# Another order of the same items in a fused gated-delta-rule and softplus kernel on one core

## The chip, the core and the metric

The kernel runs on one core of a Trainium2 chip. The metric is device time in microseconds: the median of several executions. Five instruction streams matter: PE (TensorE), DVE (VectorE), ACT (ScalarE), POOL (GpSimd) and SP (the queue that issues most loads). Each runs its own list strictly in the written order and waits where an operand is not ready or a buffer not free.

## The reference

Two layers follow each other. The first is a linear attention with a delta rule, for 4 batches x 8 heads, 768 time steps, head size 48; the second a feed-forward layer on 3072 tokens of 384 features with 2048 hidden units.

```python
k_n = k / (norm(k) + 1e-6)
for t in range(768):
    y[t] = g[t] * einsum('bhd,bhde->bhe', q[t], state)
    v_old = einsum('bhde,bhd->bhe', state, k_n[t])
    state = state + beta[t] * einsum('bhd,bhe->bhde', k_n[t], v[t] - v_old)
x = y as (3072, 384)
h = x @ w_in
out = (maximum(h, 0) + log1p(exp(-abs(h)))) @ w_out
```

## The kernel before

**Chunks.** Time is cut into 12 chunks of 64 steps. All 32 (batch, head) pairs of a chunk are worked on together. Within a chunk the recurrence is solved by a triangular inverse; between chunks only the state goes on. Chunks are paired into six groups (0 and 1, 2 and 3, and so on), and one inverse serves a pair.

**Items.** The kernel first records a list of 1286 items. An item is a small piece of work on one engine with its dependences and buffers: a load, a group of matmuls, a copy. A word in the table `_ORDER` then names an engine letter (P PE, D DVE, A ACT, G POOL, S SP) and the item's number, and `emit` issues the items exactly in that order. Buffers come from rings and are given out in the order of first use, so the order also sets which buffer an item waits for. Nothing else decides the order: there is no scheduler behind it. The names of items used below, with c for the chunk:

- `load` (lines 302 and 305): k, q, v or g of a chunk in two halves of 192 KB each, all issued by SP. The twelve buffers of one ring take them. `bload` (264) are small loads of beta, `wload` (330) the four parts each of w_in and w_out, issued by POOL and cast on the way.
- `cast` (copies at 209 to 213) makes f16 of q and of the first chunks' k; `ksq` and `red` (351 to 362) square k and sum it; `sqrt` or `pow` (368 to 374) and `eps` (381, 383) finish the norms; `kmul` (406) scales k by them.
- `trsk`, `trsq` (422, 454) transpose k and q on PE; `kev`, `qev` copy the result out (tile kqt). `gram` (516) and, for chunks 0 and 1, `gramd` (540), `gramk` and `gramq` form the products k k' and q k'; `kkc` copies and `mask` (498, DVE) take them out into tiles kk and mt.
- The inverse of a pair: `ln` and `pick` (604, 627; 597 for the first pair), `prep` (644), 15 `step`s (656 to 671) on DVE or POOL one behind the other, `ca` and `cb` (686, 688), three transposes `st.a`, `st.b`, `st.c` (714, tiles dn, td, tb), `tx`. Then per chunk `xmm` (744), `xs` (753), `tmm` (768), `td2`, `zmm` (789), `z`.
- The chain over chunks: `ks`, `qs` (826: old state times k and q), `w` (866: v minus that), `umm` (880), `u1`, `zu` (893), `u2`, `smm` (910) with `s` (924: the new state), `ymm` (936) with `y` (950: times g), `ytr` (963: transposes) and `xt` (copy of the result to the dense layer's input).
- The dense layer: `g1` (989) is a group of products of x with w_in, `soft` (1001) the softplus on ACT, `g2` (1016) four products with w_out, `o` the copy of an output tile, `store` (1035) its two stores.
- `fill` (1046): a group of four 128x512 products of the identity whose result nobody reads. The prediction calls it a warming group. 40 are recorded and 13 are in the table.

**Small and dense.** Most products of the chunks are small (48 to 64 rows and columns), the dense ones use the whole array. There are 96 `g1` and 96 `g2` groups, which the table puts between the small ones. PSUM has five buffers for the chunks' products, two for `g1` and a single one for `g2`, so a next output tile can start only when `o` has copied the last one out.

**Which engine.** Many items may go to one of several engines, and the letter in the table says which. So the table sets not only when a copy or a step runs but also where.

Of the kernel before, what the change touches and what calls it, by code (L numbers as in the profile page):

```python
# [1066 lines left out]
S26 S25 P138 P161 S33 S34 P151 A12 G4 S44 A173 S43 G2 A169 D176 P177 P174 D0 G227 A178 P188 D170 A15  # L1067
A3 S29 G1 D175 P182 A189 A171 D204 S30 S49 A190 A197 D183 P205 D206 S36 G201 A11 P158 S35 S28 D184
G9 D198 P202 G280 D203 D172 P281 A199 D200 D225 P216 G714 P210 A211 A212 G715 D226 P141 A282 P185
A187 A7 S27 S60 S59 S52 D5 P213 A217 A10 A207 S51 S50 A218 A179 P180 A214 A181 A186 G228 D229 D230  # L1070
S22 P208 A209 D231 D232 G233 D234 D235 D236 P133 S32 S24 A215 S41 D237 D238 D239 D240 D241 D242 D243
D244 D245 D248 D246 A293 D250 S23 S42 G273 A368 P369 S57 A370 S66 P145 P194 P136 P255 A247 A249 S31
S58 S17 D196 P264 D251 D195 S18 D257 A254 D256 G253 P258 A300 G8 D252 G121 D265 A260 P301 P135 G123
D294 S20 D266 S19 D274 G6 A259 P261 P716 A13 A295 A262 A263 A717 A718 P191 D192 A275 S21 P719 A720
S38 S37 D193 D302 D721 P147 A713 G122 D16 P219 S65 G315 G14 G361 G126 P725 D221 G125 D220 P722 D727
D726 G316 P728 D296 P137 D276 D297 D277 A724 A723 A729 P934 P928 A935 A929 D362 G363 P298 D299 P926
A927 S40 P278 D279 P303 A304 P308 A310 A309 P930 D306 D305 P283 A284 A285 P936 D307 D312 D364 P288
A931 D311 G365 D287 D292 P731 P932 A289 A290 A937 S39 D291 D286 D313 G124 P366 P267 A268 A269 G730
P150 P270 S67 S45 A933 D314 G317 G318 D733 A381 G319 G320 A367 D732 S46 D382 P735 A737 A736 D272
D271 P949 P950 D321 D322 G127 G323 P222 D224 P734 S68 D223 D324 D325 S73 P738 P938 A739 A740 P744  # L1080
A939 D326 D745 P940 G327 P371 P741 D746 D328 P747 G128 P164 S81 D742 A748 G329 A372 S99 D743 A941
G330 P951 D374 P970 A373 D331 P376 A388 P956 A971 G332 D379 D380 P749 D375 S74 G333 A378 D334 P958
A377 A957 D751 G383 A959 D336 P964 D338 A337 P389 S82 A335 P962 A390 D339 G342 P952 A965 S48 P343
D384 P352 S76 A341 D345 D344 G385 A953 D750 D340 P960 P346 A449 A348 S84 P942 A961 S47 A963 D347
D354 P753 A754 P349 A469 S75 P966 D450 D351 G451 A350 D755 D353 P968 S83 A967 P386 D470 S100 S98
D387 P752 P756 D758 P943 D757 G471 S53 D452 P391 A393 S54 P944 D392 A954 D395 P762 D394 D764 P396
A397 A955 P759 D760 A398 P945 D761 A946 D401 S97 P355 P972 G403 G453 A356 A969 P454 G476 S55 A357
P973 D763 A455 S56 P765 D402 G404 G405 D400 P974 A766 D399 G406 P767 A456 P358 D769 P975 G407 A360
D768 G408 P457 D359 A976 A978 S977 P770 G409 D458 G410 P771 A772 P979 S105 D773 A557 P477 D411 P774
G412 D775 A776 S62 P980 A564 D472 P780 S61 G413 A478 P777 D781 P981 D782 G414 A947 D473 P783 A784  # L1090
P459 P982 D460 D461 P992 A983 D462 D778 P474 S64 A993 P1008 D558 S92 A475 P1000 D779 A1009 P464 S89
D463 P479 A1001 P986 D468 A481 S113 D482 A466 D483 P990 D480 G415 G491 G416 G417 G418 G419 A987 D465
G420 P785 A991 D467 P988 D786 D787 P1012 G421 A989 S71 P484 G559 D424 A423 P998 S114 D422 A1013 D488
S90 D426 P1025 A485 A425 P996 P440 A486 D427 A999 P431 A997 S70 P994 G579 P1002 G645 S91 D489 A995
G430 P1004 A1003 S80 D433 A429 P1026 D432 G492 A1005 D490 G493 G494 P434 S106 A985 D428 S63 P1006
A436 A435 P1014 G495 D441 A1007 D442 P437 A1015 P789 S948 G496 G497 D438 P1010 A537 D790 D487 P1016
A439 D791 A1011 P1027 G498 D538 S69 A1017 P788 D560 P1028 G539 D499 P792 A1029 D500 P565 A793 D794
P1018 A566 D501 P795 D797 A1031 P798 P1019 G502 A1030 D800 D799 A625 P443 G561 P1020 D796 A444 D540
A445 G503 P801 P1021 D646 G504 P446 A1022 P803 D448 P1032 A802 S1024 G505 G506 D447 S72 D804 P562
S94 D805 P1033 A563 D626 P807 A809 D808 A544 P806 S79 P1034 G507 P810 P1035 A811 S115 D508 D509 D512  # L1100
A812 D511 P545 A1036 P816 A546 D510 P813 S78 D817 P1039 S107 G541 A513 D818 P572 A573 D815 P819 D576
S77 P1040 G647 A820 D575 D514 P542 A574 P1048 A543 P1060 D814 D580 A1049 D515 P547 P567 A1061 P1066
D551 A568 D550 G517 A569 D570 P1068 A1067 G518 S1037 D549 P552 G627 P1062 A1069 A548 S116 P1058 D556
D571 D554 D553 S85 A1063 D577 D578 P821 A1038 P519 P1052 A1059 P1072 S108 A1053 S86 S112 S96 P1041
A1073 P1056 A1057 D581 P1064 S87 G582 D521 G583 G584 P1042 D823 D822 A1065 P1050 D520 G585 D516
P1046 G586 A1051 P522 P528 D555 P1054 A523 D529 A524 A1047 D587 D628 P525 P825 A1043 S1045 D530 S95
# [56 lines left out]
```

## Time and profile before

| what | value |
|---|---|
| median of 3 runs | 243.78 us (242.98 to 243.94) |
| span of the profiled execution | 241.5 us |
| PE busy | 219.4 us (91%), 5020 matmuls |
| DVE busy | 161.7 us (67%) |
| ACT busy | 152.8 us (63%) |
| POOL busy | 113.7 us (47%) |
| moved by DMA | 27.57 MB, mean 114 GB/s |

The profile shows one execution. The span reaches from its first to its last instruction; the times of the runs are longer by what lies around it, and for the profiled execution itself only the span is listed. In rows of groups and of the timeline, L12 is line 12 of the kernel, "x32" a count, and what stands in square brackets is the idle time of the engine ahead of the row with what ended it. The line of a copy is that of a helper (209 for ACT, 211 and 213 for DVE and POOL), so copies are told apart by their tiles.

### The profile page before, as it was taken

How to read it: one execution, taken by the hardware profiler on the slowest of the kernel's cores; microseconds unless marked ns; L12 is line 12 of the kernel's file. 1: busy time of each engine (PE TensorE's matmuls, PEld its weight loads, DVE VectorE, ACT ScalarE, POOL GpSimd, SP SyncE). 2: the span in 40 equal slices, each digit the busy share in tenths (PEclk: the TensorE clock that was granted, in tenths of full speed). 3: DMA queues.
4: the chain of work that ended last, by engine and by line, in shares of the span. 5: the costliest groups of instructions: out<-in, count | busy, mean ns of one | idle time of the engine just before them, and what ended most of it. 6: DMA issues, size and time to landing. Idle time of an engine off the chain costs nothing.

```text
span 241.5 us, 11396 instructions
## 1 busy us (share of the span) xinstructions
PE 219.4 (91%) x5020; PEld 135.6 (56%) x5020; DVE 161.7 (67%) x368; ACT 152.8 (63%) x292; POOL 113.7 (47%) x197
## 2 busy tenths in 40 slices
PE   7645877879988999999999999999999999999983
PEld 2423455646764664556655566655565555677751
DVE  2768699888897889987899757896496310623000
ACT  5767576764982778876895767757363674143540
POOL 8740393875779778989597482016620000000000
PEclk9985599999999999999999999999999999999999
DMA  6999989999999399961889514962302311303112
GB/s 102 182 245 137 167 135 190 176 173 180 180 217 167 57 177 164 162 113 35 150 153 184 97 30 94 160 122 52 69 21 52 68 34 25 64 19 81 35 33 65
DMA packets 86833, 27.57 MB, mean 114 GB/s; under 512 B 77048, under 2 KB 86776, under 8 KB 86784
## 3 DMA queue, kind: packets, MB, share of 16 engines
q1 hardware_dynamic: 80624, 20.83, 52.6%
q0 software_dynamic: 3840, 3.17, 8.5%
q10 hardware_dynamic: 2320, 2.85, 5.2%
q8 instruction: 39, 0.64, 1.2%
q14 instruction: 10, 0.08, 0.1%
HBM read 25.26 MB, written 4.72 MB: 124 GB/s over the span
## 4 chain that ended last, share of the span: by engine, by line
PE 75%; DMA 7%; DVE 6%; SPq 4%; issue 3%; ACT 2%; POOL 1%; DVEq 0%; ACTq 0%; POOLq 0%
PE o L1016 27%; PE h L989 26%; DMA w_in<-in_moe_w_in_dram 4%; PE d L826 3%; SPq L305 3%; PE d L936 3%; PE d L516 2%; DMA f<-in_q_dram 2%; PE d L422 2%; PE d L963 2%; PE d L454 2%; PE d L880 2%; PE d L910 2%; PE d L893 2%; PE d L768 1%
## 5 line engine op out<-in xcount | busy, mean ns | idle before, releaser
L1016 PE MATMUL o<-w_out,ga 128*128 128x384 f16 x384 | 77.7, 327 | 0.7 <-ACT osb L209 0.6
L1001 ACT ACTIVATE ga<-h 128x512 f16<-128x512 f32 x96 | 56.5, 599 | 29.8 <-PE h L989 25.9
L989 PE MATMUL h<-xt,w_in 128*128 128x512 f16 (+1 forms) x384 | 74.0, 327 | 0.5 <-DMA w_in<-in_moe_w_in_dram 0.3
L989 PEld LDWEIGHTS <-w_in 128*128 128x128 f16 x384 | 34.5, 98 | 21.2 <-DMA w_in<-in_moe_w_in_dram 0.8
L1016 PEld LDWEIGHTS <-ga 128*128 128x128 f16 x384 | 33.7, 98 | 21.8 <-issue 0.8
L664 POOL TENSOR_TENSOR tmp<-nn,tt 128x78 f32<-128x78 f32 (+7 forms) x53 | 19.2, 362 | 16.1 <-DVE tt L671 13.0
L373 POOL TENSOR_TENSOR nv<-nv,half_c 128x16 f32<-128x16 f32 x8 | 23.5, 2940 | 6.6 <-DVE nv L362 6.5
L671 POOL TENSOR_TENSOR tt<-tt,tmp 128x78 f32<-128x78 f32 (+7 forms) x53 | 20.4, 385 | 4.2
L498 DVE TENSOR_TENSOR mt<-d,mask 128x256 f16<-128x256 f32 x48 | 18.2, 413 | 4.5 <-PE d L516 3.5
L209 ACT ACTIVATE kqt<-d 128x1024 f16<-128x1024 f16 (+1 forms) x18 | 18.0, 1000 | 4.8 <-PE d L454 3.6
L211 DVE CAST u<-d 128x384 f16<-128x384 f32 x20 | 10.9, 554 | 14.3 <-PE d L880 7.9
L209 ACT ACTIVATE u<-d 128x384 f16<-128x384 f32 x28 | 13.0, 490 | 11.8 <-PE d L880 5.4
L1046 PE MATMUL h<-ident 128*128 128x512 f16 x52 | 18.1, 493 | 1.7 <-DVE ident L197 1.7
L209 ACT ACTIVATE kk<-d 128x256 f16<-128x256 f32 x37 | 13.4, 386 | 6.3 <-PE d L516 5.4
L209 ACT ACTIVATE osb<-o 128x384 f32<-128x384 f32 x19 | 9.3, 492 | 9.4 <-PE o L1016 9.3
L454 PE MATMUL d<-ident,qn 128*128 128x128 f16 x96 | 8.5, 243 | 6.7 <-ACT qn L209 5.9
L950 DVE TENSOR_TENSOR yg<-d,f 128x384 f16<-128x384 f32 x24 | 12.3, 551 | 2.9 <-PE d L936 2.8
L924 DVE TENSOR_TENSOR s<-s,d 128x384 f16<-128x384 f16 x20 | 10.4, 542 | 5.7 <-PE d L910 4.3
L644 POOL TENSOR_TENSOR nn<-ln,beta_l 128x256 f32<-128x256 f16 x8 | 6.1, 780 | 14.2 <-DVE ln L627 14.2
L209 ACT ACTIVATE xt<-d 128x768 f16<-128x768 f16 x10 | 8.1, 813 | 7.0 <-PE d L963 7.0
L866 DVE TENSOR_TENSOR w<-f,d 128x384 f16<-128x384 f32 x22 | 11.3, 545 | 1.4 <-ACT xt L209 0.7
L362 DVE TENSOR_REDUCE nv<-f 128x16 f32<-128x768 f32 x12 | 11.3, 942 | 1.0 <-ACT f L351 1.0
(117 smaller groups left out, 346.7 us busy)
## 6 DMA issues: line engine op xcount, KB each, us to landing
f<-in_k_dram SPq DMA_DIRECT2D x24, 192.0 KB, 5.7
f<-in_q_dram SPq DMA_DIRECT2D x24, 192.0 KB, 5.6
f<-in_v_dram SPq DMA_DIRECT2D x24, 192.0 KB, 5.3
f<-in_g_dram SPq DMA_DIRECT2D x24, 192.0 KB, 5.3
out_dram<-osb ACTq DMA_DIRECT2D x29, 96.0 KB, 2.7
out_dram<-osb SPq DMA_DIRECT2D x19, 96.0 KB, 2.8
w_in<-in_moe_w_in_dram POOLq DMA_DIRECT2D x4, 384.0 KB, 7.9
w_out<-in_moe_w_out_dram POOLq DMA_DIRECT2D x4, 384.0 KB, 8.4
```

The costliest lines, as they stand in the source:

```text
L209: nc.scalar.activation(o, x, AF.Copy, scale=float(sign))
L362: lambda en: nc.vector.tensor_reduce(nvs().rearrange("p (a h) -> p a h", a=2), ksq.ap, mybir.AxisListType.X, ALU.add),
L373: nc.gpsimd.tensor_tensor(nvs(), nvs(), half_c[:, :NU], ALU.pow)
L454: nc.tensor.transpose(o[:, j], qn.ap[:, j].rearrange("p m d -> p (m d)"), ident)
L498: nc.vector.tensor_tensor(mt[c][m].ap[:, NP * p : NP * p + NP], gb[m].ap.rearrange("p (i b) -> p i b", i=NP)[:, :, n : n + C], mask[:, Non ...
L664: ENG[en].tensor_tensor(t, nn.ap[:, :, j : j + 1, j + 1 :].broadcast_to([P, 2, w, n]), tt.ap[:, :, :w, j : j + 1].broadcast_to([P, 2, w, n ...
L671: ENG[en].tensor_tensor(rows, rows, t, ALU.add)
L950: lambda en, m=m: nc.vector.tensor_tensor(heads(yg.ap, m), hd(yp[m].ap), heads(gf.ap, m), ALU.mult),
L989: nc.tensor.matmul(hp.ap[:, n * b : n * b + n], w_in[:, j, f * P : (f + 1) * P], xt.ap[:, j, t0 : t0 + n], start=(j == 0), stop=(j == 2),)
L1001: lambda en, hp=hp, o=gb: nc.scalar.activation(o.ap, hp.ap, AF.Softplus),
L1016: nc.tensor.matmul(op.ap[:, :DM], b.ap[:, col + c0 : col + c0 + 128], w_out[:, f, :], start=(f == 0), stop=(f == NF - 1),)
L1046: nc.tensor.matmul(hp.ap, ident, ident[:, None, :].broadcast_to([P, 4, P]))
```

## The change

Only the table is replaced. Both tables name the same 1259 items, each once (27 warming groups are left out), 13 warming groups among them. Rows of the old and of the new table around the start, around the first dense groups and at the end:

```diff
-S26 S25 P138 P161 S33 S34 P151 A12 G4 S44 A173 S43 G2 A169 D176 P177 P174 D0 G227 A178 P188 D170 A15
-A3 S29 G1 D175 P182 A189 A171 D204 S30 S49 A190 A197 D183 P205 D206 S36 G201 A11 P158 S35 S28 D184
+P147 G13 D11 D2 P138 A1 S25 D0 P161 G10 G227 G16 S26 G9 A173 D176 P174 P150 P177 S44 A169 A3 A175
+A14 A4 A12 D170 D178 S34 S33 P182 D201 P202 D204 A197 D198 A171 A203 P205 P145 A206 P210 A199 A184
...
-P150 P270 S67 S45 A933 D314 G317 G318 D733 A381 G319 G320 A367 D732 S46 D382 P735 A737 A736 D272
+A272 G365 G126 D292 G317 G318 G319 P222 D223 D224 P932 P731 D733 D732 S45 P734 P735 A381 A929 A736
...
-P1260 A1261 S1210 P1242 A1255 P1256 A1254 P1243 A1257 P1264 P1244 A1265 P1266 P1245 A1267 P1262
-A1246 A1247 P1272 A1263 P1270 A1248 P1273 A1271 P1268 A1269 P1274 P1275 A1276 A1277 A1278 P1279
-P1280 P1281 P1282 A1283 S1285 A1284
+P1256 A1261 A1257 P1243 P1264 S1204 S1254 P1244 P1266 A1265 A1255 P1245 P1262 A1267 A1246 A1248
+A1263 P1272 P1270 P1273 P1268 P1274 A1271 A1269 P1275 A1165 A1164 A1276 A1277 S1278 S1247 P1279
+P1280 P1281 P1282 A1283 A1284 S1285
```

What it comes to, read from the two tables:

- **Loads on SP.** Before: k0, k1, q2, v0, half of k3, q1, q0, q4, q3, and so on. After: k0, half of q2, k1, q0, v0, a beta load, halves of q4, g0, q2, k5, k2, q4, k3, q1, k4, then the second half of q1 (the 20th load), k3, q3, k2, g0, q3, k4.
- **Warming groups.** Before: nine ahead of `zu` of chunk 0, one (number 18 of the 40) right behind it, one behind `ytr` of chunk 0, and two among the dense groups (behind `tmm` and `ytr` of chunk 1). After: twelve ahead of `zu` of chunk 0, and one behind `ymm` of chunk 0.
- **Around the first dense group.** Before, `trsk` and `gram` of chunks 3 and 2 stand between the first `g1` groups. After, both `trsk` and `gram` of chunk 3 stand ahead of the first `g1` group; the copy `xt` of chunk 0 goes from ACT to DVE.
- **Engines.** DVE has 42 of the 90 steps instead of 32, POOL 48 instead of 58; DVE has 17 `kkc` copies instead of 11, 7 `xt` instead of 2, 5 `z` instead of 10; ACT has 20 stores instead of 29, SP 28 instead of 19.
- **Later on** the sequence on PE is nearly the same, with neighbours exchanged.

More of the change, by code (lines that the diff above doesn't have):

```diff
@@ L1072 @@
[L1072 to L1076, printed above, removed]
@@ new lines @@
+P1066 D548 A513 D516 D570 D571 P1068 A1067 A549 A1069 P821 P1052 P1058 A1053 P552 A1059 D823 P519
+D553 D515 P1062 P1050 A1063 P1042 P1046 D521 D520 D518 D822 A1051 A554 A652 D555 D556 D577 A1047
+P1056 A1043 A1057 G517 P528 P522 P1072 A1073 A524 P1064 S93 D529 D523 D530 S101 S1038 S80 S79 P1085
+A1065 P525 P825 A527 S87 S85 S104 S119 D578 P1054 S1037 S103 A526 D826 D579 P531 P824 A1055 P1076
+S977 A827 A1077 G647 G627 D532 D628 P1070 P828 A830 G580 D581 D582 G583 G584 G585 D667 A632 G586
+P1086 P1074 D533 D829 P831 D832 P834 D836 D648 D833 D835 A1075 A1071 A1045 P1087 D668 P633 P1088
```

109 lines of the change are left out of this document (54 added, 55 removed).

## Prediction

> **What bounds the kernel now.** I read the page first (its slices of the span), then the busy time by stretches, and then the timeline of the stretches that are not full. The first fence is from the page: clock granted to PE and DMA share, in tenths, 40 slices of 6 us.
>
> ```profile
> span 241.5 us, 11396 instructions
> ...
> PEclk9985599999999999999999999999999999999999
> DMA  6999989999999399961889514962302311303112
> ```
>
> ```profile
> 12.00:24.00 12.00, 6.41 (x141) 3.82 (x138) 9.20 (x33) 8.62 (x16) 2.47 (x5) 0.70 1.05 192
> 24.00:36.00 12.00, 9.88 (x255) 5.63 (x256) 9.47 (x19) 7.94 (x17) 7.76 (x10) 0.73 0.98 149
> 48.00:60.00 12.00, 10.19 (x306) 6.99 (x305) 10.49 (x26) 6.14 (x13) 8.14 (x16) 1.00 1.12 174
> 60.00:80.00 20.00, 17.99 (x502) 12.80 (x500) 17.51 (x35) 14.26 (x30) 16.23 (x18) 1.00 1.14 187
> 80.00:100.00 20.00, 19.91 (x482) 11.81 (x481) 17.87 (x38) 15.90 (x28) 16.17 (x34) 1.00 0.79 129
> 120.00:140.00 20.00, 19.98 (x445) 10.68 (x446) 16.84 (x39) 15.22 (x31) 14.73 (x22) 1.00 0.87 142
> ```
>
> The second is the busy time by stretches. Columns: stretch, length, busy time of PE, weight loads, DVE, ACT, POOL, clock, DMA share, GB/s. There are two regimes. From 80 us PE is busy 19.9 to 20.0 of every 20 us: PE itself is the bound, and an order with the same products can gain nothing there, only lose by a new wait. Before 80 us PE is not full, and the first dense group starts only at 40.5 us (its row stands below); there loads (DMA share about 1.0 from the start) and the chain of the first two chunks through ACT and DVE set the pace. So the change has to be priced at the start, and watched afterwards.
>
> **The change, part by part.** Every item appears once in both tables, with the same 13 warming groups, so the work removed and added is nothing; the tail (last four output groups, two last stores) stands in the same order. The profiled execution has a span of 241.5 us; the median of the runs is 243.78, so about 2.3 us lie around the span, in both kernels.
>
> *Loads.* Almost all loads stand at other places. What they cost is seen where the casts wait:
>
> ```profile
> 6.09 0.52 ACT L209 ACTIVATE kn<-f 128x384 f16<-128x384 f32 x1 [2.24 <-DMA f<-in_k_dram]
> 18.36 0.84 ACT L209 ACTIVATE qn<-f 128x768 f16<-128x768 f32 x1 [0.21 <-DMA f<-in_q_dram]
> 19.26 1.89 PE L454 MATMUL d<-ident,qn 128*128 128x128 f16 x16 [3.86 <-ACT qn L209]
> 26.88 1.32 ACT L686 ACTIVATE tw<-tt,mx 128x512 f16<-128x512 f32 x2
> 27.91 1.89 PE L1046 MATMUL h<-ident 128*128 128x512 f16 x4
> 28.45 1.06 DVE L714 STREAM_TRANSPOSE tb<-tw 128x512 uint32<-128x512 uint32 x1
> 29.73 0.96 PE L744 MATMUL d<-dn,kk 64*64 64x32 f16 x64
> ```
>
> The first two loads land at 6.1, the 13th (q of chunk 0) at 18.4: (18.36 - 6.09) / 11 = 1.11 us a load. In the new order q of chunk 1 is complete only with the 20th load, at about 18.4 + 7 x 1.11 = 26.1, and ACT now has its cast (0.84) directly ahead of the two copies that let the first inverse out (1.32). So these end at 26.1 + 0.84 + 1.32 = 28.3, where they end at 28.2 now, although the 15 steps of that inverse are all on DVE in the new order. The transpose st0.c starts at 28.4 as before. On PE, trsq1 (eight of the 16 products that take 1.89) runs from 27.0 to 28.0 and a warming group stands between it and xmm0; in the slow clock that group takes 1.89 us, so xmm0 starts at 29.9 (now 29.73). No gain up to here.
>
> *From xmm0 to the first dense group.* More stands in the queues of this chain:
>
> ```profile
> L209 ACT ACTIVATE kqt<-d 128x1024 f16<-128x1024 f16 (+1 forms) x18 | 18.0, 1000 | 4.8 <-PE d L454 3.6
> ...
> w_in<-in_moe_w_in_dram POOLq DMA_DIRECT2D x4, 384.0 KB, 7.9
> ```
>
> ```profile
> 26.91 1.47 POOL L353 TENSOR_TENSOR f<-f 128x768 f32<-128x768 f32 x1 [9.52 <-DMA f<-in_k_dram]
> 37.72 1.02 DVE L950 TENSOR_TENSOR yg<-d,f 128x384 f16<-128x384 f32 x2
> 39.34 1.76 DVE L406 TENSOR_TENSOR kn<-f,nv 128x768 f16<-128x768 f32 x2
> 39.34 0.81 ACT L209 ACTIVATE xt<-d 128x768 f16<-128x768 f16 x1 [0.46 <-PE d L963]
> 40.51 1.49 PE L989 MATMUL h<-xt,w_in 128*128 128x256 f16 x12 [0.34 <-DMA w_in<-in_moe_w_in_dram]
> 41.01 0.95 DVE L362 TENSOR_REDUCE nv<-f 128x16 f32<-128x768 f32 x1
> 43.58 0.69 DVE L211 COPY kqt<-d 128x1024 f16<-128x1024 f16 x1 [0.41 <-PE d L422]
> ```
>
> ACT has the copy qevq1 (1.0) ahead of td20, and DVE a transpose and a cast ahead of xs1: I put umm0 1.0 us later. The products of y0 end now at 37.72 + 1.02 = 38.7; with that 1.0 and a mask that stands between them (0.4) at 40.1. Copy xt0 goes from ACT to DVE, behind kmul2.0 (half of 1.76), red4 (0.95) and kevk2.0 (0.69): 40.1 + 0.9 + 0.95 + 0.7 + about 0.5 for itself gives 43.1, where it ends at 40.15 now. On PE the transposes of chunk 2 stand ahead of ytr0 and wait for the same kmul2.0. The first dense group starts at about 43.2, 2.7 later. Its weights come just ahead: on POOL the second w_in load stands behind the square of k4 (26th load, 18.4 + 13 x 1.11 = 32.8, and 1.47), is issued near 34.3 and takes 7.9: 42.2.
>
> *From there to umm1.* The late part is mostly work brought forward (trsk3, trsk2 and gram3 already stand before the first dense group), so I compare at umm1, which both need for chunk 1.
>
> ```profile
> 47.48 1.93 DVE L604 STREAM_TRANSPOSE ln<-kk 128x1024 uint32<-128x1024 uint32 x1
> 47.72 0.83 PE L989 MATMUL h<-xt,w_in 128*128 128x256 f16 x6
> 48.38 0.61 PE L422 MATMUL d<-ident,kn 128*128 128x128 f16 x8
> 49.29 1.04 PE L1046 MATMUL h<-ident 128*128 128x512 f16 x4
> 50.09 1.01 DVE L866 TENSOR_TENSOR w<-f,d 128x384 f16<-128x384 f32 x2
> 52.24 0.43 PE L880 MATMUL d<-w,td 64*64 64x48 f16 x31 [0.92 <-ACT kqt L209]
> 54.01 0.32 PE L516 MATMUL d<-kqt 48*64 48x64 f16 x16
> 54.16 0.42 PE L826 MATMUL d<-s,kqt 48*64 48x48 f16 x32
> ...
> 58.68 1.03 PE L1046 MATMUL h<-ident 128*128 128x512 f16 x4
> ```
>
> ```profile
> L498 DVE TENSOR_TENSOR mt<-d,mask 128x256 f16<-128x256 f32 x48 | 18.2, 413 | 4.5 <-PE d L516 3.5
> L213 DVE TENSOR_SCALAR kk<-d 128x256 f16<-128x256 f32 x11 | 4.3, 415 | 0.4 <-PE d L516 0.4
> ```
>
> DVE has from xt0 to w1.0: ten masks (10 x 0.413), three kk copies (3 x 0.415), ln2 (1.93), pick2 and eps4 (about 0.9), w1 (1.01), together about 9.2; w1.0 ends at 43.1 + 9.2 = 52.3 and umm1 at about 52.9, now 52.24 + 0.43 = 52.7. That is +0.2 to +0.3. By then PE has done one dense group (0.83) and one transpose group (0.61) less, but gramq1.1 and qs1 (0.32 + 0.42) more: +0.7. The two warming groups at 49.29 and 58.68 are gone from here (2.1 us), but the first stood in a wait: its time becomes waiting. Sum at umm1: +1.0.
>
> *53 to 80 us.* Here PE now waits 20.00 - 17.99 = 2.0 us between 60 and 80, and spends 1.03 in the second warming group. This cover can absorb the 1.0; against it stands an inverse of chunks 2 and 3 that comes out about as late as now (its ln2 starts near 47.5 in both). I take -0.5, between -1.0 and 0.
>
> *After 80 us.* SP gets nine more stores and ACT nine fewer, and SP's loads stand behind those stores, which wait for their output copies. The tightest pair I find is v of chunk 10, behind the stores of chunk 7's first output; its use by w10 stands a full chunk of dense groups later. I count 0, and nothing for the issue time that ACT saves, since PE does not wait for ACT there. DVE is the tight one: it gets 42 of the 90 steps instead of 32.
>
> ```profile
> 121.54 1.08 DVE L714 STREAM_TRANSPOSE dn<-ta 128x512 uint32<-128x512 uint32 x1
> 127.44 1.92 DVE L604 STREAM_TRANSPOSE ln<-kk 128x1024 uint32<-128x1024 uint32 x1
> ...
> 163.06 0.42 DVE L753 TENSOR_TENSOR xs<-d,mk 128x256 f16<-128x256 f32 x1
> ```
>
> ```profile
> 164.02 0.18 PE L768 MATMUL d<-tb,xs 64*64 64x32 f16 x2
> ```
>
> ln8 now starts 5.9 us after st6.a. In the new order 16 items stand between them (two transposes, six masks, three kk copies, two w, two xs, a tx): with the means above 9 us, so ln8 starts near 132 instead of 127.4. Followed down the DVE and POOL columns, the last xs8 then ends near 164.0, where it ends at 163.5 now and PE uses it at 164.02. The half microsecond of slack is gone: I take +0.3, from 0 to +4, because several such places follow one another.
>
> *The spreading.* From chunk 1's first dense group on, the places where a dense group follows a small product or a transpose number 83 in the old order and 82 in the new. I count nothing for it.
>
> Sum: +1.0 - 0.5 + 0.3 = +0.8, so 243.78 + 0.8 = **244.6 us**, practically no change.
>
> **The rivals.** *Faster, 242.2.* The clock column shows 0.70 and 0.73 between 12 and 36 us, after a wait of PE of 3.86 us (row of 19.26 above). In the new order twelve of the 13 warming groups stand before zu0 (now nine) and the longest wait of PE there is, by my column sums, 2.4 us (trsq2 waits for q2). If the clock then stays full, the group ahead of xmm0 takes 1.04 instead of 1.89 and the start loses 0.45 less; if the waits between 60 and 80 and the group at 58.68 go as well (2.0 + 1.0, of which I count 0.5 already), the sum is +0.8 - 0.45 - 2.0 = -1.6. [...] Against it: PE would still be mostly idle between 22 and 27 us in the new order, and between 24 and 36 us the mean clock was only 0.73 although PE was busy for 9.88 of 12 us, so a wait much shorter than 3.86 does not make it safe.
>
> *Slower, 247.* The DVE column after 120 us. Point from which it decides: xs8 later than 164.0, or o5.1, which is now on DVE behind the last step of inverse 8, later than 154. Each microsecond beyond goes into PE; at +3 the time is 247.
>
> *Slower, 246.* The loads: 1.11 us a load is one estimate, and q of chunk 1 is the 20th. At 1.25 it lands 1.0 us later, and the whole first chain with it; with waits for k4 and for the weights behind it +2.
>
> *The change doesn't do what it says:* the dense part is nearly the same sequence, so this is the forecast itself.
>
> **How the numbers follow.** Forecast 0.42 (own range 243.4 to 245.8), faster rival 0.22, DVE 0.24, loads 0.12. I take 0.5% (1.2 us) as what a measurement can tell. Below 242.6: 0.22. Within: 0.30 of the forecast's 0.42. Above 245.0: 0.12 + 0.24 + 0.12 = 0.48. The range, 241.5 to 248.5, reaches to the faster rival less 0.7 and the DVE rival plus 1.5.
>
> **What would show it.** First dense group at 43.2 (right: 42 to 44); umm1's end at 52 to 53.5; PE busy about 10 us of the 12 from 48 to 60, with no warming group among them; DVE's ln8 near 132; PE at 20.0 of 20 in each stretch from 80 to 220 (waits ahead of L768 or L880 there are the DVE rival). A granted clock of 1.00 between 12 and 36 is the faster rival. Wrong altogether: a first dense group before 40 or after 46.

## The result, and the profile after

The changed kernel takes **251.18 us** (250.35 to 251.40, four runs) against 243.86 us of the old one on the same chip (242.98 to 244.07): a ratio of 1.032 (95% interval 1.027 to 1.037). The forecast was 244.6 with a range that ended at 248.5. The profiled execution took 250.99 us with a span of 249.2 us. In some kernels below the runs of one order lie up to 7 us apart, the longer ones mostly at a lower granted clock (a3: 247.18 us at 0.979, 253.03 to 254.05 at 0.939 to 0.952), so every range is given and the ratios rest on the shorter runs alone.

The first lines are from the profile's page of the changed kernel: the granted clock and the DMA share in 40 slices, and one row of the DMA queues (packets, MB, share) that the prediction never looked at.

```profile
span 249.2 us, 11387 instructions
...
PEclk9989558979999999999999999999999999999999
DMA  6999999999991399980599984920101600021123
...
q8 instruction: 39, 0.64, 1.3%
```

The busy time by stretches, columns as in the prediction (stretch, length, busy time of PE, weight loads, DVE, ACT, POOL, clock, DMA share, GB/s):

```profile
24.00:36.00 12.00, 8.31 (x168) 4.87 (x167) 10.31 (x17) 6.28 (x14) 8.78 (x10) 0.54 1.18 150
48.00:60.00 12.00, 8.87 (x251) 6.21 (x250) 9.16 (x24) 6.44 (x16) 9.14 (x10) 0.86 1.34 192
60.00:80.00 20.00, 17.40 (x481) 12.98 (x481) 16.47 (x40) 13.95 (x26) 9.97 (x15) 1.00 0.91 148
80.00:100.00 20.00, 18.60 (x498) 11.88 (x492) 17.27 (x40) 14.57 (x29) 15.12 (x28) 1.00 0.70 123
140.00:160.00 20.00, 18.46 (x555) 11.70 (x544) 14.25 (x36) 9.16 (x18) 14.11 (x30) 1.00 0.79 143
```

PE is less busy than before from 24 to 36 us (8.31 against 9.88) and from 48 to 60 us (8.87 against 10.19), and, against the forecast, it is not full between 80 and 100 and between 140 and 160 us either. What ends PE's waits is in its timeline (start, length, operation, count; in brackets the wait ahead of the row and what ended it):

```profile
35.12 1.03 PE L454 MATMUL d<-ident,qn 128*128 128x128 f16 x8 [1.31 <-DVE qn L211]
...
43.81 0.24 PE L910 MATMUL d<-u,kn 64*64 64x48 f16 x5 [0.78 <-issue]
...
46.21 0.82 PE L989 MATMUL h<-xt,w_in 128*128 128x256 f16 x6
...
50.83 0.72 PE L989 MATMUL h<-xt,w_in 128*128 128x256 f16 x5 [1.38 <-issue]
...
57.30 0.21 PE L826 MATMUL d<-s,kqt 48*64 48x48 f16 x1 [1.64 <-issue]
...
63.49 0.40 PE L910 MATMUL d<-u,kn 64*64 64x48 f16 x25 [2.07 <-issue]
...
92.16 0.46 PE L936 MATMUL d<-u,mt 64*64 64x48 f16 x18 [1.10 <-issue]
...
145.32 0.59 PE L989 MATMUL h<-xt,w_in 128*128 128x512 f16 x2 [0.80 <-issue]
...
149.88 0.30 PE L789 MATMUL d<-td,kk 64*64 64x32 f16 x15 [0.74 <-issue]
```

Two things stand here. The first dense group starts at 46.2 instead of 40.5 (forecast 43.2). And from 43 us on each of PE's long waits ends with "issue": no operand was late that the profile shows. They lie in the middle of a group, ahead of its last product even (row of 57.30). The reader can find out what they have in common by counting. A window that reaches from the end of one such wait to the end of the next gives PE's products and its own weight loads (its LDWEIGHTS records):

```profile
43.81:50.83 7.02, 5.02 (x128) 3.60 (x129) 7.02 (x16) 4.11 (x11) 5.71 (x5) 1.00 1.16 193
50.83:57.30 6.47, 4.83 (x129) 3.27 (x129) 3.94 (x9) 2.36 (x5) 3.90 (x6) 0.74 1.33 198
57.30:63.49 6.19, 4.12 (x128) 3.18 (x128) 4.08 (x15) 4.13 (x8) 5.51 (x8) 1.00 1.37 177
92.16:149.88 57.72, 55.88 (x1409) 32.71 (x1409) 49.55 (x108) 42.01 (x81) 39.60 (x65) 1.00 0.82 142
```

128 + 128 = 256 each time (one or two more where an edge counts twice), and 2818 = 11 x 256 + 2 over the long stretch. Queue q8 moves 0.64 MB in 39 packets, 16.4 KB each; PE's 5020 products and 5020 weight loads are 39 times 256 and a rest, so there is about one packet for 256 of them. I call such a block of 256 of PE's instructions a **page** and the place between two of them a page edge; that a packet of q8 is the fetch of the next page is my reading of these counts and of the times below. In the list of all of PE's records, counted from 0 and with the two to four records of its sequencer that stand ahead, the first product behind each wait has number 1218, 1474, 1730, 1986, 3522, 6081 and 6337 (another run can have the same edge one record earlier or later). Over 0.4 us there are no other waits of PE between 36 us and the last output group; together these seven are 8.5 us of a span of 249.2. The old kernel has two such waits at the same spacing (0.58 and 0.76 us, at 1473 and 2753):

```profile
47.53 0.25 PE L826 MATMUL d<-s,kqt 48*64 48x48 f16 x9 [0.58 <-issue]
...
73.02 0.35 PE L893 MATMUL d<-u,z 64*64 64x48 f16 x21 [0.76 <-issue]
```

When a page comes late is seen in the packets of q8. In the view of the DMA queues (packets, MB, share of the 16 engines in the window) the page needed at 49.4 us has not begun until 48.2 us, although the page before it began at 43.81; loads fill the engines:

```profile
q0 software_dynamic: 542, 0.50, 69.6%
q1 hardware_dynamic: 1055, 0.33, 40.0%
```

```profile
q0 software_dynamic: 197, 0.15, 80.8%
q1 hardware_dynamic: 186, 0.09, 38.7%
q8 instruction: 1, 0.02, 5.5%
```

(The first fence is 43.81 to 48.2 us, the second 48.2 to 49.4; q0 carries the loads of w_in and w_out that POOL issues, below "loads of the weights", q1 the loads that SP issues.) Taken for several pages from the same packets and from PE's records:

| kernel, page at number | page before began | fetch began (later by) | PE ran on | PE's wait |
|---|---|---|---|---|
| before, 1473 | 41.06 | 45.08 (4.02) | 47.53 | 0.58 |
| before, 1729 | 47.53 | 48.58 (1.05) | 53.43 | 0 |
| before, 1985 | 53.43 | 53.89 (0.46) | 57.74 | 0 |
| after, 1474 | 43.81 | 48.28 (4.47) | 50.83 | 1.38 |
| after, 1730 | 50.83 | 54.41 (3.58) | 57.30 | 1.64 |
| after, 1986 | 57.30 | 60.77 (3.47) | 63.49 | 2.07 |

In these rows a fetch starts only after the page before has begun, and where PE waits it runs on 2.4 to 2.9 us after the start of the fetch. In the last three rows PE had used up the page before 5.64, 4.83 and 4.12 us after it began, sooner than the delay and this time together (7.02, 6.47 and 6.19).

**The sum.** Products of `ymm0` end 3.1 us later (40.8, before 37.7). Behind that, page waits grow by 8.51 - 1.34 = 7.2, PE's other waits over 0.4 us fall from 3.15 to 0, and two warming groups fewer stand there (2.1). 52.3 to 55.7 us run at half clock with PE busy (rows below), about 1.7 by my estimate, half of that stretch. 3.1 + 7.2 - 3.15 - 2.1 + 1.7 = 6.8 of the 7.7 us of the spans. This is an account of one pair of profiles; what each term costs the end is asked below.

**What delays `ymm0`** is seen beside each other on DVE and POOL in the changed kernel (castq3 and eps2 on DVE; ksq2, ksq4 and kmul3.0 on POOL):

```profile
31.54 3.52 DVE L211 CAST qn<-f 128x768 f16<-128x768 f32 x1
...
40.42 1.39 DVE L381 TENSOR_SCALAR nv<-nv 128x16 f32<-128x16 f32 x1
```

```profile
31.59 2.90 POOL L353 TENSOR_TENSOR f<-f 128x768 f32<-128x768 f32 x2
...
40.31 1.47 POOL L406 TENSOR_TENSOR kn<-f,nv 128x768 f16<-128x768 f32 x1 [3.12 <-DVE nv L383]
```

Both operations of DVE last until those of POOL beside them have ended: the cast until 35.06 (POOL's squares 34.49), eps2 until 41.81 (kmul3.0 41.78). I call this the lock; the word is a name for what these rows show. The clock adds to it: the changed kernel is at half clock from 24.98 to 38.63 us, the old one only until 30.47 (from 16.82), and the warming group between `umm0` and `zu0` (36.64) takes 1.89 us, where the same group at 40.69, at full clock, takes 1.04.

### The profile page after: what moved, and what is told of

It reads as the page before. It is cut to its first block, busy times and chain, and to the rows that moved or that the text cites. A ratio compares the mean times of both kernels' runs of the same rounds, so it can differ in the third digit from the quotient of the medians.

```text
span 249.2 us, 11387 instructions
## 1 busy us (share of the span) xinstructions
PE 222.0 (89%) x5020; PEld 137.3 (55%) x5020; DVE 169.5 (68%) x387; ACT 151.1 (61%) x293; POOL 109.1 (44%) x177
## 4 chain that ended last, share of the span: by engine, by line
PE 75%; DVE 7%; SPq 6%; issue 5%; ACT 3%; DMA 2%; DVEq 0%; ACTq 0%
PE h L989 26%; PE o L1016 25%; SPq L305 3%; PE d L826 3%; PE d L516 3%; PE d L936 2%; DMA f<-in_q_dram 2%; PE d L454 2%; PE h L1046 2%; SPq L302 2%; PE d L744 2%; PE d L893 2%; PE d L422 2%; PE d L768 2%; PE d L880 1%
## 5 line engine op out<-in xcount | busy, mean ns | idle before, releaser
L1001 ACT ACTIVATE ga<-h 128x512 f16<-128x512 f32 x96 | 56.6, 600 | 28.5 <-PE h L989 25.1
L989 PEld LDWEIGHTS <-w_in 128*128 128x128 f16 x384 | 35.5, 98 | 24.0 <-issue 3.3
L209 ACT ACTIVATE u<-d 128x384 f16<-128x384 f32 x31 | 14.1, 489 | 16.4 <-PE d L880 11.6
L664 POOL TENSOR_TENSOR tmp<-nn,tt 128x126 f32<-128x126 f32 (+7 forms) x43 | 15.4, 358 | 15.9 <-DVE tt L671 13.2
L209 ACT ACTIVATE kk<-d 128x256 f16<-128x256 f32 x31 | 11.2, 386 | 14.5 <-PE d L516 9.1
L671 POOL TENSOR_TENSOR tt<-tt,tmp 128x126 f32<-128x126 f32 (+7 forms) x43 | 16.7, 388 | 3.4
L211 POOL COPY tx<-tb 64x512 f16<-64x512 f16 x8 | 4.9, 607 | 20.6 <-DVE tb L714 16.1
L211 DVE CAST u<-d 128x384 f16<-128x384 f32 x17 | 9.2, 551 | 6.4 <-PE d L893 4.7
L664 DVE TENSOR_TENSOR tmp<-nn,tt 128x110 f32<-128x110 f32 (+7 forms) x41 | 10.6, 258 | 4.3 <-POOL tt L671 3.1
L406 POOL TENSOR_TENSOR kn<-f,nv 128x768 f16<-128x768 f32 x8 | 11.8, 1474 | 3.6 <-DVE nv L383 3.1
L516 PE MATMUL d<-kqt 48*64 48x128 f16 (+1 forms) x448 | 11.3, 218 | 1.9 <-ACT kqt L209 0.9
```

Of the source, the lines that this page charges most:

```text
L209: nc.scalar.activation(o, x, AF.Copy, scale=float(sign))
L211: ENG[en].tensor_copy(o, x)
L516: nc.tensor.matmul(gb[m].ap.rearrange("p (i b) -> p i b", i=NP)[HALF[r], i, lo:hi], x[:, :C], x[:, lo:hi],)
L664: ENG[en].tensor_tensor(t, nn.ap[:, :, j : j + 1, j + 1 :].broadcast_to([P, 2, w, n]), tt.ap[:, :, :w, j : j + 1].broadcast_to([P, 2, w, n ...
L671: ENG[en].tensor_tensor(rows, rows, t, ALU.add)
L989: nc.tensor.matmul(hp.ap[:, n * b : n * b + n], w_in[:, j, f * P : (f + 1) * P], xt.ap[:, j, t0 : t0 + n], start=(j == 0), stop=(j == 2),)
```

## The experiments

"Page waits" are PE's waits of over 0.4 us at page edges between 36 and 235 us, from the profile.

### Which half of the table: h1, h2

`h1` takes the old table up to and with group g11.14 (word P970) and then all remaining words in the new order; `h2` the other way round. Each has 13 warming groups.

> The old table up to and with the group g11.14 (60 us), then the rest in the new order; 13 warming groups as in the old table. Theory 'start': of the 7.4 us that the new order loses, 5.8 are lost ahead of g11.14 (66.0 against 60.2 us in the two traces) and 1.5 to 2 behind it, so this kernel takes 245 to 246. Rival 'late': the lost time ahead of 66 us would be caught up by waits that go, and the loss is made behind it: 248 or more. In the trace PE's waits of 0.7 to 1.1 us at 256-instruction distances (see below 'fetch') are expected behind 80 us at the same places in the instruction stream as in the new order.

> The new table up to and with g11.14, then the rest in the old order. Theory 'start': 249 to 250 (5.8 of the 7.4 kept). Rival 'late': 246 or less. The two hybrids together should add up: (this - before) + (the other hybrid - before) = about 7.4 if the two parts are independent.

h1: 248.31 us (245.49 to 250.15), ratio 1.0135 (1.004 to 1.023). h2: 251.08 (250.03 to 251.38), ratio 1.028 (1.021 to 1.035). The start carries most of it. 1.35% + 2.8% is more than 3.2%, but by less than the intervals (about 1.2 and 0.5 points), so whether the halves add stays open. By its time h1 lies between the two theories (245 to 246, and 248 or more), and h2 lies above the 249 to 250 of the first. h2 has page waits of 8.6 us, also at 2498 and 2754; h1 has those at 6082 and 6338 (0.83, 1.22) as expected. Neither theory foresaw h1's wait of 2.83 us ahead of xmm2 (below, h1p).

### The lock: a1, a2

```diff
 a1: castq3 (300) from DVE to ACT, behind td20
-G121 D300 P264 G5 A259 A260
+G121 P264 G5 A259 A260 A300
 a2: ksq2 (273) behind td20 and ksq4 (361) behind u20, on ACT
-G273
+A273
-G361
+A361
```

> The new order, with one copy (cast of q of chunk 3) on ACT as in the old one, behind td20, instead of DVE, where it took 3.52 us beside two squares on POOL. Theory 'lock' (DVE's copy from SBUF to SBUF is held up by POOL's operations): the cast takes 0.84 on ACT, the wait of 1.31 ahead of trsq3 goes, xs1, red3, red2 and umm0 come 2 to 3 us earlier, the first dense group at 43.5 to 44.5 instead of 46.2, and the time falls by 1.5 to 2.5, to 249 or so. Rival 'fetch' (PE waits for its next 256 instructions, at instruction numbers that lie a multiple of 256 apart, which came 2.5 to 4.5 us late while the loads ran): the gain at umm0 is there, but PE stops at the same instruction numbers again and the time stays within 0.7 of 251.2.

> The new order, with the cast of q3 left on DVE, and the squares of k2 and k4 moved from POOL to ACT (0.8 us each there). Theory 'lock': the cast takes 0.5 to 1.5 us instead of 3.52, since no long operation of POOL stands beside it. Rival: the cast is slow for itself (its data or its tile): 3 us or more again, with POOL empty beside it.

In a2 the cast takes, as expected, less than 1.5 us: with no square of POOL beside it, it takes 0.70; eps2, here ahead of kmul3.0, takes 0.16:

```profile
31.83 0.70 DVE L211 CAST qn<-f 128x768 f16<-128x768 f32 x1 [0.44 <-DMA f<-in_q_dram]
...
39.49 0.16 DVE L381 TENSOR_SCALAR nv<-nv 128x16 f32<-128x16 f32 x1
```

So the same cast takes 3.52 us beside POOL's squares of 2.90 us and 0.70 without them, and the lock is shown for this cast and these squares. Why the cast lasts so long, the rows do not show. But a2 took 250.98 in its one run: its first dense group starts at 44.6, 1.6 us earlier, and nothing is gained at the end. In a1's profile the first dense group starts at 43.0, 3.2 us earlier, and the page at 1730 then makes PE wait twice as long as before:

```profile
53.16 0.21 PE L826 MATMUL d<-s,kqt 48*64 48x48 f16 x1 [3.33 <-issue]
```

a1's runs: 246.34 (granted clock 0.979) and 250.93 to 252.78 (0.944 to 0.970). One run lies below both theories, the other three near or above the rival's 251.2. What the cast costs the end lies between nothing and 4.8 us; this pair does not settle it. Nor need the 3.2 us at the first dense group be the cast's alone: a1 is at half clock for only 3.41 us twice between 19.6 and 29.8, while a1f1 and a3 below, with the same cast on ACT, are at half clock until 38.7 and 40.4 and reach their first dense group at 45.6 and 47.2.

### Traffic taken away from the fetch, and added: f1, bf1, d1, b2

```diff
 f1 (new table), bf1 (old table): small loads of late chunks
+            if c >= 6 or (c == 5 and name != "k"):
...
+                ENG[en].dma_start(
+                    out=b.ap[64 * b2 : 64 * b2 + 64, 0, 0],
+                    in_=x[2 * b2, 0, t0 : t0 + C],
+                )
+                return
 d1 (old table): behind the loads of q5, v2 and k6, twice each
+            ENG[en].dma_start(
+                out=extra[2 * EXTRA[name, c, b2] + h],
+                in_=k[2 * h : 2 * h + 2, :, :C].rearrange("p h t d -> t (p h) d"),
+            )
 b2 (old table): on POOL behind step2.4, three times; wload w1.3 ahead of them
+            nc.gpsimd.dma_start(
+                out=extra[i],
+                in_=moe_w_out.rearrange("(j p) n -> p j n", p=P)[:, 4 * i : 4 * i + 4],
+            )
```

In f1 and bf1, q, v and g of chunk 5 and everything of chunks 6 to 11 are loaded only in small part, so these chunks compute on what their buffers held. The extra transfers of d1 and b2 go to a scratch place in memory.

> The new order, with the loads of chunks 6 to 11 and of q, v and g of chunk 5 cut to a small part (the rest of the buffer keeps what an older chunk left there, so these chunks compute on other data). The weights and all other work stay. Theory 'fetch behind loads' (the fetch of PE's next 256 instructions waits in the DMA engines behind loads; it began 4.47, 3.58 and 3.47 us after the page before had begun, for the pages at PE instruction 1474, 1730 and 1986): these delays fall to 1 to 2.5 us, the waits of 1.4, 1.6 and 2.1 there to below 0.7 each, those at 3522, 6082 and 6338 (1.1, 0.8, 0.7) to nearly nothing, and the time to 244 to 247. Rival 'density' (PE runs through a page of small products faster than a page can be fetched, however idle the DMA is): the same waits at the same numbers, 250 to 251.

> The control: the old order with the small loads of the late chunks alone. The theory lets it gain little, since only one of its page waits (0.8 at 2753) is behind such loads: 242 to 243.5, so that the distance of the two orders falls from 7.4 to 3 to 4. Rival (less traffic helps both alike): 238 to 240.

f1: **246.59 us** (244.76 to 247.89, eight runs), ratio 1.0148 (1.010 to 1.019): 1.7 points, 4.2 us, less than the new order, with the same table and the same late start (first dense group at 46.5). Page waits fall from 8.5 to 4.1, also by 4.4. All behind 62 us are gone, and PE is full there:

```profile
80.00:100.00 20.00, 19.95 (x476) 12.16 (x475) 18.02 (x40) 16.94 (x34) 15.61 (x28) 1.00 0.33 65
140.00:160.00 20.00, 20.00 (x483) 12.51 (x485) 16.10 (x41) 12.12 (x22) 11.54 (x27) 1.00 0.21 43
```

Those at 1474, 1730 and 1986, where the weights still move, stay, against the 0.7 us that was expected as their most (starts and lengths from the chain that ended last):

```profile
49.76 1.24 issue
54.47 1.35 issue
59.95 1.51 issue
```

The control bf1, the old order with the same cut, takes 241.41 (241.11 to 244.22), ratio 0.994 (0.990 to 0.999): 1.4 us, with page waits of 1.5 against 1.3. So 2.8 of the 4.2 us are the new order's own, give or take 2.0 by the three intervals. bf1's wait at 2753 stays (0.60): its page was fetched only 0.73 us late, but PE ran on 3.05 us after the start of the fetch. So a page wait was measured here without a late fetch.

> The old order, with six extra transfers of 192 KB (k of chunk 0, to a scratch place in memory that nobody reads) behind SP's loads of q5, v2 and k6, which are issued between 47 and 58 us. Theory 'fetch behind loads': in the old order the pages at PE instruction 1729, 1985 and 2241 were fetched 1.05, 0.46 and 1.99 us after the page before began; with the extra traffic these become 2.5 to 4, PE waits 0.5 to 2.5 us at one or more of these numbers (now 0), and the time rises by 2 to 5 us to 246 to 249. Rival: the fetch does not share anything with the loads: no wait at these numbers, time within 1 us of 243.5, or later only by waits for landed data (v2, k6).

> The old order with three extra transfers of the form of the weight loads (a part of w_out, cast on the way, to a scratch place in memory that nobody reads), issued by POOL in its idle stretch at 55 to 57 us; the last real weight load is moved ahead of them. Theory 'fetch behind weights': pages that begin between 55 and 66 us (instructions 2241 and 2497; fetched 1.99 and 1.28 us after the page before began) are fetched 3 to 4.5 us after, PE waits 0.5 to 2 at one or both, time 245 to 247. The run with extra loads on SP's queue had no such wait. Rival: no wait at these numbers, 243 to 244.

d1: 249.61 (two runs), ratio 1.025 (1.013 to 1.037), but **not** by the fetch: no page wait at 1729, 1985 or 2241 (fetches 1.05, 0.92 and 1.08 late). Most of the time went into a late load of q5, a chain that the views of PE and ACT show (the page wait at 2753 grew too, from 0.76 to 1.25):

```profile
65.45 0.80 PE L1002 MATMUL h<-xt,w_in 128*128 128x256 f16 x3 [4.82 <-ACT ga L1014]
```

```profile
64.07 0.84 ACT L209 ACTIVATE qn<-f 128x768 f16<-128x768 f32 x1 [5.20 <-DMA f<-in_q_dram]
```

So "behind loads" is not borne out, but the test is a weak one: in the two microseconds after these three pages began the DMA share was 0.75, 1.25 and 1.28 (before: 0.53, 0.83 and 1.47). b2, with transfers of the weights' form, has the wait: the page at 2497 is fetched 4.09 us late, and PE waits 1.83 in the middle of an output group, after 257 records:

```profile
70.73 0.32 PE L1018 MATMUL o<-w_out,ga 128*128 128x384 f16 x1 [1.83 <-issue]
```

```profile
64.03:70.73 6.70, 4.88 (x129) 3.62 (x128) 5.64 (x11) 4.13 (x7) 4.46 (x4) 1.00 1.21 192
```

It took 248.45 (two runs), ratio 1.020 (1.011 to 1.029), more than the 245 to 247 expected: 6.8 us of half clock follow the wait, and 3.4 stand ahead of it. Over the pages of all 20 profiles whose fetch began after the page before, it began 0.9 us later on average where nothing else moves in the two microseconds after that page's start (123 pages), 1.8 with only the other queues at a share over 1 (113), and 3.6 with the loads of the weights at a share over 0.9 (27).

### Loads of the weights earlier: w1, w2

POOL issues w0.2 and w0.1 right behind w0.0, w1.0 and w1.1 behind ksq4, and w0.3 behind kmul3.0 (w2); w1 has castq3 on ACT besides.

```diff
-wloadw0.0 pad2.2 ksq2 ksq4 wloadw0.2 clear4 diag2 kmul3.0 wloadw0.1 wloadw1.0 wloadw0.3
+wloadw0.0 wloadw0.2 wloadw0.1 pad2.2 ksq2 ksq4 wloadw1.0 wloadw1.1 clear4 diag2 kmul3.0 wloadw0.3
```

> The new order with two things put back: the cast of q3 on ACT, and POOL issues the weight loads earlier, about where the old order does (three before the squares of k2 and k4, two right behind them). Theory 'lock and fetch behind loads': first dense group near 43 (as in the run with the cast alone), fewer weight bytes move between 44 and 60 us, so the pages at 1474, 1730 and 1986 come earlier, their waits sum to below 2 us instead of 5, time 245 to 248. Rival: the sum of traffic is the same, so the waits stay: 249 to 252.

> The new order with only the weight loads issued earlier on POOL. Theory: first dense group at about 46 as before the edit, waits at the pages at 1474 to 1986 sum to 2 to 3 instead of 5, time 248 to 249.5. Rival (traffic only moved): 250 to 252.

w1: 250.30 (248.69 to 251.01), ratio 1.027 (1.020 to 1.034); w2: 249.73 (248.25 to 254.19), ratio 1.024 (1.015 to 1.032). In w1 no wait over 0.4 is left at 1474, 1730 and 1986, as the theory said, and yet nothing is gained: 1.66 us come back ahead of the first dense group, 2.4 at the pages at 2498 and 2754, 1.9 at 6081 and 6337. In w2 (profile of its longest run) PE waits 4.50 ahead of trsk3, and the waits at 1474 to 1986 sum to 3.7, not to 2 to 3. So w1's time is the rival's (249 to 252) and its waits moved; w2's lies between its theory (248 to 249.5) and its rival (250 to 252), and both are above the old order.

### Small w_out: f2, f3, bf, f4, f5

```diff
 f2; f3 and bf with f1's cut besides (new, new, old table)
-                    lambda en, dst=dst, src=src: nc.gpsimd.dma_start(out=dst, in_=src))
+                    lambda en, dst=dst, src=src, which=which: nc.gpsimd.dma_start(out=dst, in_=src)
+                    if which == 0
+                    else nc.gpsimd.dma_start(out=dst[:, 0, :D], in_=src[:, 0, :D]))
...
+    prog.after = lambda: nc.gpsimd.memset(w_out, 0.0)
 f4; f5 with f1's cut besides (new table)
+                nc.gpsimd.memset(dst, 0.0)
+                nc.gpsimd.dma_start(out=dst[:, 0, :D], in_=src[:, 0, :D])
```

These kernels load only 48 of the 1536 columns of each part of w_out (a 32nd, not the 24th of the expectation) and set the rest to zero.

> The new order, with the four loads of w_out cut to one 24th of a part (the rest of w_out is set to zero by POOL in an idle stretch near 15 us, so the output is another). The loads of k, q, v, g stay. By all pages of the runs so far, PE's page fetch begins 0.7 us after the page before when nothing is loaded, 1.9 with loads of k, q, v, g at a DMA share over 1.1, and 3.7 when weight loads have a share over 0.9. Theory 'fetch behind weights': in 50 to 64 us, where w_out's parts were moving, the waits at instructions 1730 and 1986 (1.6 and 2.1) fall below 0.7 each; that at 1474 (w_in still moving) and those at 3522, 6082, 6338 stay; time 247 to 248.5. Rival 'fetch behind the other loads': waits as in the new order, 250 to 251.

> The new order with both cuts: small loads of the late chunks, and small w_out. Theory 'fetch behind loads and weights': no wait at a page boundary over 0.7 behind 50 us, only the one at 1218 or 1474 with w_in; the time falls to 243 to 245, and the distance to the old order with the same cuts (the next kernel) is what the order costs without the fetch: 1 to 3 us, from the first chunk's chain (the cast held up on DVE). Rival: the order itself is slow, distance 6 to 8 as without the cuts.

> The old order with the same two cuts. It has few waits at page boundaries (0.6 at 1473, 0.8 at 2753), so by the theory it gains 0.5 to 1.5: 242 to 243. By the rival that less traffic helps any order by its earlier data, it gains as much as the new order, 5 or more.

f2: 254.94 (252.72, 257.15); f3: 248.63 (247.14 to 249.91), ratio 1.021 (1.013 to 1.028); bf: 240.99 (240.47 to 244.14), ratio 0.989 (0.983 to 0.994). The page waits did what the theory said (f2: none over 0.4 at 1730 and 1986; f3: 0.8 in all; bf: none), the times did not: f3 and bf lie 3.2 points (7.6 us) apart, as far as the two orders with all their loads. By the times f3's rival, that the order itself is slow, came true. My zeros are the reason for part of it: in f2's profile (its longer run) a copy of DVE ahead of the first inverse lasts 5.97 us, until POOL's memset of 5.22 us beside it has ended (19.93 and 19.88), and the first dense group starts at 50.7 (f2) and 50.8 (f3); in bf no DVE operation lasts so long beside the memset, and the group starts at 39.6:

```profile
13.96 5.97 DVE L641 COPY tt<-bl 128x32 f32<-128x32 f32 x1
```

```profile
14.66 5.22 POOL L1067 MEMSET w_out<- 128x6144 f16 x1
```

So f4 and f5 set the zeros part by part.

> The new order with the loads of w_out cut as before, and the zeros now set by POOL part by part where the loads stood (42 to 64 us; 1.3 us each by 5.22 / 4), so that the first inverse is not disturbed. What it leaves out: most of w_out. Theory 'fetch behind weights': first dense group at 46 to 47 as in the new order; the waits at instructions 1730 and 1986 (1.6 and 2.1) fall below 0.5 each, that at 1474 stays at 1 to 1.7 (w_in moves there); time 247 to 249. Rival (other loads): waits stay, 250 to 252.

> The same with the small loads of the late chunks too (q, v, g of chunk 5 and all of 6 to 11). Theory: no wait at a page boundary behind 52 us; time 243.5 to 246, below the 246.3 of the run with small loads alone. Rival: no gain from w_out's part, 246 to 247.

f4: 250.19 (249.55 to 250.87), ratio 1.031 (1.024 to 1.038); f5: 247.84 (247.05 to 248.22), ratio 1.020 (1.013 to 1.026). The theory failed here in size. In f4 the fetches at 1730 and 1986 start earlier (1.93 and 2.65 late instead of 3.58 and 3.47), but PE, not held up at 1474 any more, reaches these edges earlier too, and still waits 0.98 and 1.76. In f5 the page waits are down to 0.7, and other waits stand in their place, 5.0 in all: the largest is 1.73 ahead of xmm2, the inverse of chunks 2 and 3. f5's first dense group starts at 45.7, 6.1 us behind bf's, and its ratio is still 3.1 points above bf's (whose zeros are set elsewhere): with the page waits nearly gone the late start is not made up for.

### What lies under the page waits: h1p, a1f1, a3

h1p is h1 with `pow5` (383) and `eps5` (384) moved behind the steps of that inverse; a1f1 is a1 with f1's small loads; a3 is a1 with the same move.

```diff
 POOL
-step2.10 step2.11 clear4 pow5 step2.12 tx2.0
+step2.10 step2.11 clear4 step2.12 pow5 tx2.0
 DVE
-diag4 eps5 mask4.10 step2.13
+diag4 mask4.10 step2.13
-st2.c xs2.1
+st2.c eps5 xs2.1
```

> The hybrid of the old start and the new rest, with one thing put back: POOL's square roots of chunk 5 (pow5, 3.3 us) and the eps behind them stand behind the steps of the inverse of chunks 2 and 3, as in the old order, not ahead of step 12. In the hybrid DVE waited for step 12 from 61.2 to 65.1 and PE 2.84 us ahead of xmm2 (65.31 to 68.15), with 6.8 us of half clock behind it. Theory: this wait goes, st2.a at 64 (was 67.0), time 245 to 246; what is left over the old order is the waits at 6082 and 6338 (0.8 and 1.2). Rival: the rest of the new order is slow elsewhere, 247.5 or more.

h1 (profile of its longest run), where POOL's square roots (2.94 us and 0.26) hold DVE's eps5 and step 12 of the inverse, and through them PE:

```profile
60.94 2.94 POOL L373 TENSOR_TENSOR nv<-nv,half_c 128x16 f32<-128x16 f32 x1
```

```profile
64.27 0.25 DVE L383 RECIPROCAL nv<-nv 128x16 f32<-128x16 f32 x1 [3.06 <-POOL nv L374]
```

```profile
68.15 0.62 PE L744 MATMUL d<-dn,kk 64*64 64x32 f16 x32 [2.83 <-DVE dn L714]
```

In h1p the wait is gone, and the time is 246.28 (244.09 to 246.84), ratio 1.010 (1.003 to 1.018), 2.0 us below h1 by the medians but only 0.3 points by the ratios, less than their intervals, and between the theory (245 to 246) and the rival (247.5 or more). Page waits are 3.4 (0.8 and 0.7 at 6082 and 6338, and 1.4 at 1985, which h1 had not).

> The new order with the small loads of the late chunks, and the cast of q3 back on ACT. If the held-up cast costs the end what it costs the first dense group (46.2 against 43.0 us), and the fetch does not eat it: 243 to 244, 2.5 to 3.3 below the run with small loads alone. Rival 'pages set the pace between 36 and 66 us whatever the chain does': within 1 us of 246.3.

> The new order with the cast of q3 on ACT and pow5 put back. All the traffic is there. Theory 'pages set the pace between 36 and 66 us': first dense group at 43, but the waits at 1474 to 1986 sum to 4 to 5 again and the time is 248 to 250.5. Rival 'chain': with cast and pow5 right, the inverse of chunks 2 and 3 comes 4 us earlier than in the new order and the time falls to 245 to 246.5.

a1f1: 246.84 (243.77 to 247.67), ratio 1.012 (1.002 to 1.022), no different from f1's 246.59, with a first dense group at 45.6 and page waits of 4.4 (f1 4.1): the rival. a3: 253.11 (247.18, and 253.03 to 254.05), outside both ranges; the profile is of its longest run, with page waits of 5.6 (3.27 at 1730) and the first dense group at 47.2, not the 43 expected. Even its shortest run is 4.1 us above the 243.05 of the old order beside it: putting the chain right does not bring the new order back by itself.

## Why the prediction was wrong, step by step

- **"From 80 us PE itself is the bound ... an order with the same products can ... only lose by a new wait."** The first half failed. PE had 18.60 and 18.46 of 20 us in two stretches, and the new wait was of a kind not on my list: its own instructions (1.10, 0.80, 0.74). f1, where all waits behind 62 us are gone at a DMA share of 0.33 and 0.21 in these stretches (0.70 and 0.79 in the changed kernel), shows that traffic in the DMA engines is behind it.
- **"The spreading ... I count nothing for it."** By the sum above this is the step that cost most: the term put at nothing measured 7.2 us (page waits of 8.51, before 1.34), of which other waits gave back 3.15. I counted places where a dense group follows a small product (83 and 82) and saw no difference. What counted here is how long a page of 256 lasted on PE (4.12 to 5.64 us ahead of the three longest waits), and what the DMA engines carried just then (page waits of 8.5 us fell to 4.1 in f1, and one of 1.83 came in b2). The old profile had the sign, two waits put down to issue at 47.5 and 73.0 us.
- **"Loads"** was right within 1.0 us: castq1 25.4 (forecast 26.1), end of the copies 27.4 (28.3), st0.c 27.5 (28.4), xmm0 28.9 (29.9). Part of the difference is the count: the 20 loads hold the small one of beta, and 19 would have given 25.1 for castq1.
- **"I put umm0 1.0 us later"** was too little: 36.1 instead of 34.7. The term named the cast ahead of xs1 but gave it too little: it took 3.52 beside POOL's squares (0.70 in a2). y0 ended at 43.4 (40.1): eps2 took 1.39 instead of 0.16 in the same way, and the warming group between umm0 and zu0 ran at half clock (1.89 us). The steps behind it were sized well: y0's end to xt0's end took 2.8 (3.0).
- **"Sum at umm1: +1.0"** became +5.1 (57.8 against 52.7): 3.0 from the late first dense group, and PE stood at the page edge from 55.66 to 57.30 right ahead of umm1.
- **"53 to 80: this cover can absorb the 1.0"** failed; the page wait of 2.07 lies there.
- **The DVE rival** did not come: the last xs8 ends at 170.0 and tmm8 starts at 170.9, 0.8 us of slack (0.5 before) in a kernel that is 7 us late. **The loads rival** did not come. **The clock rival** was wrong the other way: 0.54 between 24 and 36 us (rows below). Its sum has a slip besides: 2.0 + 1.0 less the 0.5 already counted is 2.5, not 2.0.
- **The weights.** I followed the second w_in load through POOL's column but not those after it. POOL issues w0.1, w1.0 and w0.3 at 41.7 to 43.3 (before: 33.0, 36.9 and 47.5), so that they move while PE works through pages of small products.

**What stays open.** That traffic makes page waits here is shown by taking it away (f1, 8.5 us to 4.1) and adding it (b2, a wait of 1.83), the lock by a2 (3.52 and 0.70), and h1's wait of 2.83 behind pow5 by h1p. How the 7.3 us divide among them is not settled: f5 has nearly no page waits and is still 2.0% above the old order and 3.1 points above bf, a1 gains 3 us at the first dense group and not surely any at the end, and w1 moved the waits instead of removing them. That each sets the pace where the others let go would fit all of these, but no run shows it. Why fetches began later beside loads of the weights than beside the other loads (3.6 and 1.8 us on average), nothing here shows. No version found beats the old order with all of its work.

## What to carry to other kernels

Where PE waits for "issue" in the middle of a group, count its products and weight loads between two such waits: here the waits stood a multiple of 256 of PE's records apart, within one, all seven of the changed kernel and both of the old one. An operand that comes earlier did not help there (a1's wait at 1730 doubled, 3.33 against 1.64); less traffic at that time did (f1, 8.5 us to 4.1). Whether larger products there help, no run tested. Before moving a copy to DVE, look at what POOL runs beside it (the cast took 3.52 and 0.70). A chain that a change shortened gained here only until the next limit (a1, f5), so ask what stands right under it.

## What the runs showed of the hardware

**Instruction pages.** 19 of the 20 profiles have such waits over 0.4 us, all at the same numbers modulo 256 (within one; 193 and 194 in the old and the changed kernel). Where the fetches of 16.4 KB began after the page before, they did so on average 0.9 us later with no other traffic, 1.8 with the other queues at a share over 1 and 3.6 with the loads of the weights at a share over 0.9 (all 20 profiles); beside loads of the weights it was up to 5.4 us (a3, from 44.29 to 49.67).

**The clock.** In the changed kernel it is half from 11.32 to 14.74, from 24.98 to 38.63 and from 52.28 to 55.70 us (3.41, 13.65 and 3.41 us), and full from 14.74 to 24.98 and from 38.63 to 52.28 (10.24 and 13.65). The rows are stretches of 3.41 us of this kernel:

```profile
21.54:24.95 3.41, 1.62 (x40) 1.16 (x40) 3.00 (x13) 3.41 (x7) 0.00 (x0) 1.00 1.20 194
24.98:28.39 3.41, 2.13 (x12) 1.29 (x12) 2.90 (x5) 2.45 (x5) 1.44 (x2) 0.50 1.37 158
...
35.22:38.63 3.41, 3.41 (x56) 1.78 (x59) 2.54 (x5) 1.19 (x4) 0.87 (x3) 0.50 0.87 140
...
48.87:52.28 3.41, 1.92 (x70) 1.34 (x58) 3.29 (x6) 2.00 (x6) 3.41 (x3) 1.00 1.23 190
52.28:55.70 3.42, 3.38 (x89) 2.12 (x87) 1.01 (x3) 1.67 (x4) 2.45 (x5) 0.50 1.36 201
55.70:59.11 3.41, 1.81 (x72) 1.52 (x75) 3.20 (x10) 1.29 (x3) 1.69 (x1) 1.00 1.47 176
```

At 24.98 and 52.28 the clock fell after stretches in which PE was busy for 1.62 and 1.92 us, the longest single wait in the second being 1.38, and came back after those with 3.41 and 3.38. But the stretch with PE busy for 1.81 us (55.70 to 59.11), with the page wait of 1.64 in it, was followed by the full clock, which then stays to the end of the work: PE's busy time alone gives no rule here. Half clock follows a page wait at 52.28 here (the wait of 1.38, over at 50.83), and in b2 at 71.76 (the wait of 1.83, over at 70.73); behind the waits of 1.64 and 2.07 here the clock stayed full. What sets it, these runs do not show.
